# One order table for another in a fused attention and feed-forward kernel: the same operations and tiles, replayed in a new order on every engine

## Chip, cores and metric

The kernel runs on one core of a Trainium2 chip. The metric is the device time of one execution in microseconds (us), the median of several runs.

## What is computed

The inputs are q, k and v of 8 batches, 12 heads, 448 positions and 64 features, and two weights, w_in (768 x 2048) and w_out (2048 x 768), all in float32. Attention has no softmax: the scores are cut at zero, squared and divided by the sequence length. Its output, with the heads side by side, is 3584 rows of 768, and goes through a feed-forward block.

```python
def _attn_ref(q, k, v):
    S = q.shape[2]
    scale = 1.0 / np.sqrt(q.shape[-1])
    scores = scale * np.matmul(q, k.transpose(0, 1, 3, 2))
    attn = np.maximum(scores, 0.0) ** 2 / S
    return np.matmul(attn, v).astype(np.float32)

def _moe_ref(x, w_in, w_out):
    h = x @ w_in
    g = 0.5 * h * (1.0 + erf(h / np.sqrt(2.0)))
    return (g @ w_out).astype(np.float32)
```

## The kernel before

**Stages.** The work goes batch by batch, and the feed-forward work of earlier batches is laid between the attention work of later ones, so that TensorE always has some of either. All matmuls are in bf16.

- *Loads.* GpSimd's queue (POOL) loads q, k, v and the weights, casting to bf16 (`load_q` L501/L506, `add_k` L585/L588, `add_v` L608, `load_win` L521 to L523, `load_wout` L527). Its loads share eight semaphores in turn, so a load waits until the one eight places ahead has landed. w_in comes in five pieces of columns (`WINS`). The first pieces of q and k come through other queues.
- *Transposes.* For batches 0 and 1, TensorE turns q (`add_tq` L696) and k (`add_tk` L667) into PSUM tiles `tp`, and VectorE or ScalarE copies them out to `qT` and `kT` (`copy`, L548 on VectorE, L550 on ScalarE). For later batches SyncE's queue transposes by DMA.
- *Attention.* QK^T (`fn_qk`, L806, into `ps`), relu with scale (`fn_relu`, L823 on ScalarE, L825 on VectorE), square (`fn_mul`, L833 on ScalarE, L835 on VectorE), and the product with v (`add_av`, L885, into `pav`), which collects the seven blocks of 64 positions of k; its two halves are copied to `xT` (L548/L550). Batch 0 is worked in two halves of 224 positions of q, half 0 first; this shows as 64x224 matmuls. A half-width relu works on 128x448.
- *Feed-forward, first GEMM.* For half of batch 0 and a few column blocks, plain products of 12 matmuls (`add_f1`, L947, into `psh`) and a gelu (L957). For all else a seven-product scheme on 2 x 2 blocks: TensorE's products (`pe`, L1103; `pb`, L1256 for the last batch), sums of weights and of x on VectorE (`ws` L1018, `t_x` L1062), passes out of PSUM (L1141 on VectorE, L548/L550) and the gelu (L1153).
- *Feed-forward, second GEMM.* 14 groups of 256 rows (`add_group`), each with seven products in the same scheme (`pso`, L1432), sums of h on VectorE (`s_sb`), additions on VectorE into `osb` (L1466) and stores by SyncE (L1385, L1393). In the last group the last product is written in two parts, columns 0 to 255 and 256 to 383 of the half (`LAST = 256`), each with an addition and a store of its own.

Ahead of it all stand nine matmuls on zeros, 512 wide (`spin`, L1567), and a few more are put among the early work (`fill`, L1577).

**Tiles.** PSUM tiles come from two pools: `w` has three of two banks, `f` two of one bank. The bf16 attention tiles `a_sq` come from 14 buffers of pool `a`.

**What sets the order.** Every piece of work is an operation of the class `Scheduler` (`add`), numbered as it is added, with the engines that can do it. `place` replays the string `ORDER`: each word is a letter and an operation's number. P or Q puts it on TensorE, A on ScalarE, D on VectorE, G on POOL, S on SyncE, and Z places a fill. Q also changes the operation's PSUM tile: transposes take a `w` tile instead of an `f` tile, and QK^T and the product with v take two `f` tiles instead of one `w` tile. The order of the words is the order in which each engine issues its instructions. The string `HOMES` gives the buffer, in turn, that each tile of a pool takes. Waits follow from data and from buffers: an engine issues in order, and what stands behind a waiting instruction waits too.

```python
for word in ORDER.split():
    ...
        op, eng = self.open[int(word[1:])], names[word[0]]
        if word[0] == "Q":
            op.split()
    ...
    self.commit(max(self.ready(op), free), op, eng, dur, lat)
```

Of the kernel before, what the change touches and what calls it, by code (L numbers as in the profile page):

```python
# [84 lines left out]
0120120120120121210210210201201201201201201201202012010021210011021201201201021012102021021200221121  # L85
2201201201200120210210202020010212002102102102102121011001121010201012012012012010110011220112012012
021211000101201210212012021
""".replace("\n", ""),
    "f": """
0101010101010101011010101011010101010101011011010101010010101010101010101010101010101001010100110101  # L90
01010
""".replace("\n", ""),
    "a": """
0123456789abcd32105649c8b297301a546d89c723b14605ada8c91734526d0a918b652c74301abd98c6b2a50419d3879483
d174725ac60b893d271064ba53c893c210a74d3a89a37405628bc14d29a8564db03718078313d710b52a8c49670532d20985
7b137987357398a06c14d2a7359b57b259aa760814cd39b264513c807ba
# [3 lines left out]
D16 G3 G2 Q17 D18 A13 P14 D15 A19 Q20 D21 P22 D23 P45 D46 P42 A43 P39 G4 G7 P24 A40 D25 P32 D33 P36  # L100
D37 P57 A58 Z1024 Q51 A52 Q28 D41 D29 D44 Q34 D35 D59 A47 G10 Q30 A31 P54 A55 G6 P26 D27 P99 P84 A85
Z672 P69 A70 Q72 D38 D53 D56 P60 A61 D100 D62 D71 A73 G5 P48 A49 P66 D50 A67 D68 P114 A115 Q87 A88
G121 P78 A79 D116 D74 P96 D97 G8 P63 A64 G9 Q75 A65 A76 A77 P93 D94 P111 P105 A106 D112 D113 D80
D107 A95 G11 P144 A145 P108 A109 P81 A82 A83 G120 Q132 P134 D133 G12 P146 A147 D135 P167 A168 P161
A162 D86 D89 D110 P179 D180 D98 D101 P148 A149 P90 A91 D92 G129 P173 A174 D169 G125 G124 Q136 D137
Q164 A165 P102 A103 A104 D175 P117 D118 A119 P170 D171 D172 D253 P138 A139 D163 D166 D181 D254 P176
A177 D178 P245 A246 P194 A195 P185 A186 D187 P200 G123 G128 A201 P150 A151 P249 A250 P197 D198 D199
P188 A189 P191 A192 P142 P140 P203 A204 D141 G122 P182 D143 P209 A210 A183 D205 D193 D196 P215 A216
A184 P247 A248 P251 A252 P212 A213 P221 A222 G127 G126 D190 D202 P206 A207 A208 Q224 G131 P261 P278
D257 D258 P218 A279 D255 D225 A262 A219 G152 G153 Q227 A228 P268 P285 A269 D256 P264 P281 D214 A282  # L110
A265 P263 P280 D223 A211 D217 D259 P273 D260 P270 P287 G130 A220 D226 D229 D266 D286 D288 A289 Q230
A231 A232 D271 P276 P293 D283 D274 A277 A294 D374 P290 D375 D377 P378 D291 P395 A396 A379 P380 P385
P402 A275 A386 A403 A284 D376 D412 D415 P397 D400 D383 A272 P381 P398 D413 A382 P407 A399 D408 P416
P433 D434 A401 P404 P390 G240 G241 D450 P387 D391 A292 A384 D388 D405 A417 A392 A409 P419 P436 A437
A389 P423 P440 A420 A441 D414 G243 D453 D457 P410 A267 D458 P393 A411 A394 S233 P425 P442 D443 S234
Q302 A424 D426 P314 A315 A427 A303 P445 P428 P431 D429 A430 P418 D446 D451 D459 A432 Q308 A309 A444
P317 A318 P435 D438 D421 D454 P448 A449 D456 D460 D319 P462 A463 P305 A306 P311 P320 A321 A322 P464
A316 D465 P466 P468 D452 D304 D461 G155 G156 G158 G159 G239 A312 A467 S236 S235 P329 A406 A330 A313
P341 A342 D469 D455 P335 D336 D310 D307 A439 P470 D471 P472 P326 D327 S238 A447 A422 D494 S237 P368
A369 P350 A351 D495 P474 D475 P362 G242 G154 P323 G157 G160 A363 D473 D324 P344 D328 D352 A345 D346  # L120
A325 A337 D331 D496 P353 A354 D355 D497 P498 A499 P500 D501 P338 A339 D340 D343 P359 P332 A333 D334
G244 G295 G296 G297 S478 S476 A364 A360 A370 P502 D503 P504 D505 P356 A361 P347 A348 A349 D357 A358
P365 D366 D367 P506 D507 S479 P532 P523 A524 P526 D527 A533 P508 P514 D515 D516 D525 P520 A521 P371
A372 A373 D586 P529 P517 A518 A530 P510 D528 P590 A522 P607 A608 D587 D589 P597 D511 D531 P592 P614
A615 D591 D588 P609 D595 A596 G298 P593 P619 D612 P610 P626 A598 D624 P602 A611 D620 A594 P643 A627
A534 A644 G299 G300 G484 S481 S482 S483 S477 A613 D603 A604 A621 P616 P599 D617 D600 A601 P628 P645
D648 D631 D509 A618 P629 A632 D630 P622 D625 P605 P633 P650 D651 A623 A606 P646 P635 A634 S480 P547
Q538 A539 D676 A548 P655 P638 D636 D647 D519 D639 A640 P641 P652 P556 D656 A657 A557 D653 P544 D545
G487 G301 Q535 G490 G485 G486 D536 P568 G488 G489 G491 G492 A642 A654 P541 A542 D677 P658 A659 D540
D537 P680 D681 A569 A549 D678 D543 S662 D570 P565 D566 S512 P574 A575 P553 A554 A555 P682 P684 D683  # L130
A685 P550 A551 S660 S513 P562 P577 A563 A578 A649 A637 S663 S661 G666 G669 P686 D546 D558 D552 P688
D687 D689 P580 D581 P571 G493 P559 A572 A576 A560 P716 P734 A735 A561 P690 D679 P692 D579 D717 D696
D697 A567 A564 A718 D691 D699 D693 S695 P728 P722 A729 P719 A720 A723 P700 D701 P702 D721 D573 A582
P704 P740 A741 D703 P731 D732 D705 A724 P583 A584 A585 P749 D750 A736 P725 A726 A727 P708 P792 P809
D698 P794 P706 P811 D788 D733 D751 D742 D789 P799 P816 A817 A810 D730 D707 D709 P712 A793 D800 P710
D814 D791 P795 A796 D713 A815 D797 A798 P804 D711 P821 D805 P812 D813 P752 D822 A753 Q737 P743 A744
P755 A756 A757 D790 P801 P818 D819 P828 P845 A829 A823 A846 A738 A739 P830 D802 P824 P847 D826 D827
P831 P848 D850 D833 A851 A803 D832 D849 S665 S664 Q764 G672 G667 G668 G670 P835 P852 P837 P854 G671
G673 G674 A825 A806 A765 A745 P807 A808 D836 D853 D838 D855 A856 P840 P857 D841 A839 A842 D878 D858
D879 D880 P843 P860 A844 A861 P882 A859 A883 P746 A747 P773 P770 D771 D772 D766 S715 S862 S714 S864  # L140
S865 P884 D885 A774 D775 P758 S866 S863 P933 P930 A931 D754 P886 D887 A748 D934 G868 G871 G675 P888
P890 D889 D881 A834 A820 A759 D898 D891 P892 D893 S896 P927 D928 D929 P779 A935 A760 A780 D781 P761
A762 A763 P782 D783 P767 D900 D899 P902 A903 P894 D895 D932 A768 D769 A784 P776 A777 P924 D925 D926
P954 A955 A778 S867 S694 G874 G869 G870 P906 P904 D905 P936 D937 P918 A919 G872 G873 G875 A938 G876
P785 D786 D787 P921 A922 D901 P948 P908 A907 P945 A946 D992 D909 A923 P960 A956 A961 A949 P910 D911
D990 P912 P914 D920 D913 D991 D915 P994 A995 D950 P942 A943 A944 Q966 D967 P939 P957 A958 Q951 P1011
D993 P997 S1067 P1001 P1018 A1002 A1019 S916 S1065 G1070 G1073 S1064 S1066 S897 G877 D940 D941 D998
P996 D1012 P1013 D1016 D999 A1000 P1014 D1015 P1023 P1006 D1007 P1030 P1047 P1003 A1008 A968 D1024
A1025 P1032 D1048 P1049 D1028 D1052 A1031 A959 D1035 A1036 P1020 D1021 P1033 P1050 A1051 A1034 A1017
D1004 D1029 D952 D953 P1037 P1054 P1026 A1053 A1055 P1039 P1056 A1038 D1040 D1057 P1009 A1010 A1058  # L150
A1027 P1042 P1059 A1005 D1043 D1060 P1045 P1062 A1046 A1063 A1044 A1041 P1084 A1085 D1080 P969 P978
A979 D1082 P984 A985 D1081 P1086 D970 P1088 D1083 D1087 P1090 A962 A1061 A947 D1091 P972 P1138 A1139
A1022 D973 D974 D971 A986 P963 A1089 A980 P1135 A1136 P975 D964 D976 D965 P1094 D1095 P1092 D1093
P981 A982 P1144 A1145 P1126 A1127 D1100 D1101 D1137 D983 P1104 P1096 D1097 S1099 P1153 D1154 A977
P1159 A1160 P987 A988 A989 P1123 D1124 P1150 A1151 P1106 D1105 P1132 A1133 P1120 A1121 P1129 D1130
P1108 D1107 S917 D1122 D1152 D1102 D1103 D1109 D1161 A1140 A1134 A1155 P1196 P1198 P1215 P1213 A1197
D1201 A1214 P1110 S1069 G1076 S1068 S1098 G1071 G1072 P1112 D1111 D1218 A1219 D1113 A1125 D1192
D1193 P1114 G1074 G1075 G1077 D1115 D1131 D1194 A1128 P1116 D1117 P1162 A1163 D1146 P1141 A1142
D1195 P1168 D1169 Q1147 A1148 A1149 A1143 P1199 P1216 D1170 G1078 S1271 D1200 P1203 P1220 Q1186
D1217 P1156 A1204 A1221 A1187 A1157 P1222 P1205 D1230 D1164 D1206 A1202 D1223 A1224 P1225 P1208  # L160
D1209 A1210 D1226 P1232 P1249 D1250 P1228 D1231 P1234 P1251 A1233 A1188 D1237 D1254 P1235 P1252
A1229 D1253 P1211 P1239 P1256 A1227 A1238 A1255 A1212 D1236 P1241 P1258 D1240 D1242 A1158 A1207
A1257 D1259 A1243 P1180 D1181 A1260 Q1174 A1175 P1244 P1261 P1247 D1262 A1263 P1264 A1265 A1248
# [1607 lines left out]
```

## Time and profile before

| what | value |
|---|---|
| median of 3 runs | 357.82 us (357.68 to 358.1) |
| the profiled execution | 357.81 us, its span 356.04 us |
| TensorE (PE) busy | 348.8 us, 98%, 3853 matmuls |
| VectorE (DVE) busy | 305.4 us, 86% |
| ScalarE (ACT) busy | 269.0 us, 76% |
| mean granted TensorE clock | 1.000 |

The span runs from the first instruction to the last. The profile calls the engines PE (matmul), PEld (its weight loads), DVE, ACT, POOL and SP. A timeline row holds the start in us, the length in us, the engine, the line, the operation, the tiles, a count of instructions in a row (x20), and in brackets the idle time ahead with what ended it. A row by form holds the busy time in us, the mean in ns of one, and the idle time ahead.

### The profile page before, as it was taken

Reading aid. Unit: us, or ns where it says so; the run is one execution under the profiler, and the core shown is the slowest. Engines: PE = TensorE matmul, PEld = TensorE weight load, DVE = VectorE, ACT = ScalarE, POOL = GpSimd, SP = SyncE. Lnnn points to the kernel's source line nnn. Section 1 sums busy time; section 2 is a strip of 40 time slices with the busy share of each in tenths; the row PEclk is TensorE's granted clock in tenths of the full one; section 3 lists DMA queues with packets and bytes.
Section 4 is the critical chain, followed back from the end, with each engine's and each line's share of the span. In section 5 each row is a group of like instructions: output and inputs, shape, how many; then the busy total and the mean of one; then the engine's idle time right before and its main releaser. Section 6 shows DMA issues by size and latency. Waiting matters only on the chain.

```text
span 356.0 us, 9239 instructions
## 1 busy us (share of the span) xinstructions
PE 348.8 (98%) x3853; PEld 249.7 (70%) x3853; DVE 305.4 (86%) x514; ACT 269.0 (76%) x442; POOL 103.3 (29%) x138
## 2 busy tenths in 40 slices
PE   8899999999999999999999999999999999999995
PEld 4577689855589556786557965669669856888663
DVE  4999999999989998779988979898998799588662
ACT  4999987999978999498787798879986896412500
POOL 8665814195346102901093100290001000000000
PEclk9999999999999999999999999999999999999999
DMA  9999999999999956997699900799309103020222
GB/s 172 200 203 204 184 184 183 162 153 149 200 154 113 184 79 98 124 181 94 132 117 176 175 2 0 186 119 168 37 2 182 22 0 129 8 89 2 88 90 88
DMA packets 123465, 43.01 MB, mean 121 GB/s; under 512 B 100896, under 2 KB 120096, under 8 KB 123424
## 3 DMA queue, kind: packets, MB, share of 16 engines
q0 software_dynamic: 84432, 22.47, 66.9%
q1 hardware_dynamic: 38448, 19.50, 26.0%
q8 instruction: 30, 0.49, 0.6%
q10 hardware_dynamic: 544, 0.46, 0.4%
q14 instruction: 11, 0.09, 0.1%
HBM read 45.61 MB, written 11.01 MB: 159 GB/s over the span
## 4 chain that ended last, share of the span: by engine, by line
PE 93%; ACT 4%; DMA 1%; DVE 1%; issue 0%; DVEq 0%
PE pso L1432 37%; PE pe L1103 30%; PE ps L806 10%; PE pav L885 9%; PE pb L1256 5%; ACT a_sq L823 3%; PE psh L947 2%; DMA k<-in_k_dram 1%; ACT a_sq L833 1%; PE tp L667 0%; PE tp L696 0%; ACT h_sb L957 0%; DVE kT L548 0%; DVE nk L548 0%; ACT xT L550 0%
## 5 line engine op out<-in xcount | busy, mean ns | idle before, releaser
L823 ACT ACTIVATE a_sq<-ps 128x896 bf16<-128x896 f32 (+1 forms) x135 | 108.3, 863 | 9.7 <-PE ps L806 9.6
L1432 PEld LDWEIGHTS <-s_sb 128*128 128x128 bf16 x456 | 43.0, 98 | 31.5 <-issue 4.3
L835 DVE TENSOR_TENSOR a_sq<-a_sq 128x896 bf16<-128x896 bf16 x106 | 61.7, 617 | 1.7 <-ACT a_sq L823 1.0
L1103 PEld LDWEIGHTS <-win_sb 128*128 128x128 bf16 x624 | 59.2, 98 | 3.7 <-issue 2.8
L833 ACT ACTIVATE a_sq<-a_sq 128x896 bf16<-128x896 bf16 (+1 forms) x63 | 58.2, 950 | 0.9 <-DVE a_sq L825 0.6
L825 DVE TENSOR_SCALAR a_sq<-ps 128x896 bf16<-128x896 f32 (+1 forms) x51 | 50.6, 1003 | 3.4 <-PE ps L806 2.8
L1141 DVE TENSOR_TENSOR part<-pe,part 128x448 f32<-128x448 f32 x78 | 45.3, 619 | 8.0 <-PE pe L1103 7.3
L806 PE MATMUL ps<-qT,kT 64*64 64x448 bf16 (+1 forms) x756 | 49.1, 337 | 1.2 <-ACT a_sq L823 0.6
L1153 ACT ACTIVATE h_sb<-part 128x448 bf16<-128x448 f32 x78 | 42.6, 579 | 8.4 <-DVE part L1141 7.9
L1432 PEld LDWEIGHTS <-h_sb 128*128 128x128 bf16 x336 | 31.7, 98 | 23.4 <-issue 4.8
L1103 PEld LDWEIGHTS <-ws 128*128 128x128 bf16 x468 | 44.5, 98 | 2.1 <-issue 1.1
L1432 PE MATMUL pso<-wout_sb,h_sb 128*128 128x384 bf16 x224 | 41.1, 326 | 0.0
L1432 PE MATMUL pso<-t_sb,s_sb 128*128 128x384 bf16 x224 | 41.1, 326 | 0.0
L1432 PE MATMUL pso<-wout_sb,s_sb 128*128 128x384 bf16 (+2 forms) x232 | 41.0, 321 | 0.0
L588 POOL DMA_DIRECT2D nk<-in_k_dram x36 | 34.7, 969 | 11.3 <-DMA kT<-nk 5.1
L885 PE MATMUL pav<-a_sq,v_sb 64*64 64x448 bf16 (+1 forms) x756 | 36.3, 329 | 0.5 <-ACT a_sq L823 0.4
L550 ACT COPY part<-pe 128x448 f32<-128x448 f32 x52 | 26.0, 539 | 14.0 <-PE pe L1103 10.1
L806 PEld LDWEIGHTS <-kT 64*64 64x64 bf16 x756 | 19.7, 105 | 21.7 <-issue 15.2
L1103 PE MATMUL pe<-t_x,win_sb 128*128 128x224 bf16 x312 | 34.8, 259 | 0.0
L1103 PE MATMUL pe<-xT,win_sb 128*128 128x224 bf16 x312 | 34.5, 259 | 0.0
L1103 PE MATMUL pe<-t_x,ws 128*128 128x224 bf16 x312 | 34.0, 259 | 0.0
L506 POOL DMA_DIRECT2D nq<-in_q_dram x36 | 30.0, 838 | 10.8 <-DMA wout_sb<-in_moe_w_out_dram 10.3
(73 smaller groups left out, 399.3 us busy)
## 6 DMA issues: line engine op xcount, KB each, us to landing
out_dram<-osb SPq DMA_DIRECT2D x19, 384.0 KB, 2.9
nq<-in_q_dram POOLq DMA_DIRECT2D x37, 112.0 KB, 5.8
nk<-in_k_dram POOLq DMA_DIRECT2D x36, 112.0 KB, 5.0
v_sb<-in_v_dram POOLq DMA_DIRECT2D x5, 672.0 KB, 7.9
v_sb<-in_v_dram POOLq DMA_DIRECT2D x9, 224.0 KB, 7.1
win_sb<-in_moe_w_in_dram POOLq DMA_DIRECT2D x8, 192.0 KB, 9.2
wout_sb<-in_moe_w_out_dram POOLq DMA_DIRECT2D x1, 1536.0 KB, 15.2
wout_sb<-in_moe_w_out_dram POOLq DMA_DIRECT2D x4, 384.0 KB, 18.7
```

The costliest lines, as they stand in the source:

```text
L506: nc.gpsimd.dma_start(nq[b][:, g0, :, e], rows)
L588: nc.gpsimd.dma_start(nk[b][:, g0, :, e], rows[:, e].rearrange("p (i d) -> p i d", d=D))
L806: nc.tensor.matmul(side(ps, e)[64 * j : 64 * j + 64, x * w : x * w + w], kT[r, g, i * 128 + 64 * j : i * 128 + 64 * j + 64], moving, start ...
L823: A.activation(to, x, AF.Relu, scale=c_att)
L825: V.tensor_scalar(to, x, c_att, 0.0, op0=mybir.AluOpType.mult, op1=mybir.AluOpType.max,)
L833: A.activation(ar, ar, AF.Square)
L835: V.tensor_mul(ar, ar, ar)
L885: nc.tensor.matmul(side(pav[0], e)[o2 : o2 + 64, :w], vt[b][r, 2 * g + e, bass.ts(i, D)], box["a2"][r, e, o : o + w], start=(i == 0), stop ...
L1103: nc.tensor.matmul(bank[name][:, y, z * HS : z * HS + HS], w[:, k, bass.ts(mm, 128)], right()[:, k], start=first and k == 0 and z == 0, st ...
L1141: V.tensor_add(get(to), ps(name), get(other))
L1153: A.activation(h_ring()[:, m : m + 2, o + half[c].start : o + half[c].stop], src().rearrange("p (x n) -> p x n", x=2), AF.Gelu,)
L1432: nc.tensor.matmul(box[bank][:, n0:n1], left()[:, kf], right()[:, kf, n0:n1], start=bool(need) and kf == 0, stop=kf == K2 - 1, skip_group_ ...
```

## The change

The two tables `HOMES` and `ORDER` (L83 to L190) are replaced by others; no other line differs. Both orders have the same 1618 words, with the same operations; what differs is their order, the engine where two can do an operation (A or D), and the letter P or Q of a few. "Distance between packets" is a setting of the search that wrote the table, and is not in the kernel. One line of the diff:

```diff
 ORDER = """
-D16 G3 G2 Q17 D18 A13 P14 D15 A19 Q20 D21 P22 D23 P45 D46 P42 A43 P39 G4 G7 P24 A40 D25 P32 D33 P36
+G2 A13 A19 D16 P17 D18 Q20 D21 P14 D15 G3 Q22 D23 P45 P36 D46 Z672 G4 P24 D25 A37 D38 P32 A33 P42
```

Of the operations that two engines can do, 35 squares move from ScalarE to VectorE and 34 the other way, 32 relus from VectorE to ScalarE and 31 the other way, and some copies and passes. On TensorE the sequence changes 51 times from attention to feed-forward work and 51 times back, in both orders.

**VectorE's start.** The rows are the first copies of batch 0: `nk` is k in bf16, `tp` the PSUM tile of a transpose, `kT` and `qT` where it is copied to. Before:

```order
L548 CAST nk<-k_92 128x2x256
L548 COPY kT<-tp 128x512
L548 COPY qT<-tp 128x2x224
L548 COPY kT<-tp 128x384
L548 COPY kT<-tp 128x896
L825 TENSOR_SCALAR a_sq<-ps 128x2x224
```

And now:

```order
L548 CAST nk<-k_92 128x2x256
L548 COPY kT<-tp 128x512
L548 COPY kT<-tp 128x384
L548 COPY qT<-tp 128x2x224
L548 COPY kT<-tp 128x896
L825 TENSOR_SCALAR a_sq<-ps 128x2x224
```

The copy of q changed places with that of k's second part; on TensorE the transposes of that part likewise stand ahead of q's.

**ScalarE's start.** The rows run from the first relu to the first copies of `pav` to `xT`. Before:

```order
L823 ACTIVATE a_sq<-ps 128x896 x3
L823 ACTIVATE a_sq<-ps 128x448 x2
L833 ACTIVATE a_sq<-a_sq 128x2x224
L550 COPY qT<-tp 128x2x224
L823 ACTIVATE a_sq<-ps 128x896 x4
L823 ACTIVATE a_sq<-ps 128x448 x2
L550 CAST xT<-pav 128x224
L823 ACTIVATE a_sq<-ps 128x896
L823 ACTIVATE a_sq<-ps 128x2x224
L823 ACTIVATE a_sq<-ps 128x448 x2
L823 ACTIVATE a_sq<-ps 128x896
L550 CAST xT<-pav 128x224 x4
```

And now, from behind the q copy and the relus that lie ahead:

```order
L823 ACTIVATE a_sq<-ps 128x448 x2
L823 ACTIVATE a_sq<-ps 128x896 x2
L823 ACTIVATE a_sq<-ps 128x448 x2
L550 CAST xT<-pav 128x224
L823 ACTIVATE a_sq<-ps 128x896
L823 ACTIVATE a_sq<-ps 128x2x224
L823 ACTIVATE a_sq<-ps 128x896
L823 ACTIVATE a_sq<-ps 128x448 x2
L823 ACTIVATE a_sq<-ps 128x896
L823 ACTIVATE a_sq<-ps 128x448 x2
L823 ACTIVATE a_sq<-ps 128x896
L550 CAST xT<-pav 128x224 x3
```

Ahead of the last run of `xT` copies, two half-width relus (128x448 x2) have come in, the small square (L833) and one `xT` copy have gone.

**POOL's loads.** The rows are those of q and k of batch 1 (`nq`, `nk`) and the pieces of w_in behind them; 3x256 is the narrow piece, 3x512 the columns that a plain product reads next. Before:

```order
L501 DMA nq<-in_q_dram 112x4x256 x2
L585 DMA nk<-in_k_dram 128x2x448
L521 DMA win_sb<-in_moe_w_in_dram 128x3x512
L522 DMA win_sb<-in_moe_w_in_dram 64x3x512
L523 DMA win_sb<-in_moe_w_in_dram 64x3x512
L585 DMA nk<-in_k_dram 128x2x448
```

And now:

```order
L501 DMA nq<-in_q_dram 112x4x256
L521 DMA win_sb<-in_moe_w_in_dram 128x3x256
L522 DMA win_sb<-in_moe_w_in_dram 64x3x256
L523 DMA win_sb<-in_moe_w_in_dram 64x3x256
L585 DMA nk<-in_k_dram 128x2x448
L521 DMA win_sb<-in_moe_w_in_dram 128x3x512
L522 DMA win_sb<-in_moe_w_in_dram 64x3x512
L523 DMA win_sb<-in_moe_w_in_dram 64x3x512
```

The narrow piece and a load of k came ahead of the 3x512 piece.

**TensorE's end.** The rows are where the last product's two parts meet (`s_sb` is the sum of h, `pso` its PSUM tile). Before:

```order
L1432 LDWEIGHTS s_sb
L1432 MATMUL pso<-wout_sb,s_sb 128x256
L1432 LDWEIGHTS s_sb
L1432 MATMUL pso<-wout_sb,s_sb 128x128
L1432 LDWEIGHTS s_sb
```

And now:

```order
L1432 LDWEIGHTS s_sb
L1432 MATMUL pso<-wout_sb,s_sb 128x128
L1432 LDWEIGHTS s_sb
L1432 MATMUL pso<-wout_sb,s_sb 128x256
L1432 LDWEIGHTS s_sb
```

The 128-wide part moved ahead of the 256-wide one; their additions and stores follow that order.

More of the change, by code (lines that the diff above doesn't have):

```diff
@@ L105 @@
[L105 to L114, printed above, removed]
@@ L185 @@
[L185 to L187 removed]
+G2 A13 A19 D16 P17 D18 Q20 D21 P14 D15 G3 Q22 D23 P45 P36 D46 Z672 G4 P24 D25 A37 D38 P32 A33 P42
+A43 P39 D40 P51 A52 D44 D41 Z1024 Q96 A97 G6 Q26 P54 D27 P57 A58 G7 P28 D29 D47 Q34 D35 D53 A55 D56
+Q69 A70 G5 P48 G10 A49 D50 P60 A61 P114 A115 D71 P30 D31 P99 A100 D62 P66 P72 D73 D59 D74 Q93 P111
@@ new lines @@
+S1119 P1141 A1142 A1143 Q1147 P1168 A1169 D1193 D1195 P1216 P1199 D1194 D1148 D1149 P1203 P1220
+A1200 P1156 S1266 Q1186 A1221 D1217 P1222 P1205 A1157 A1202 A1219 D1204 D1223 A1224 D1206 P1208
+P1225 D1226 P1232 P1249 A1187 D1209 P1228 P1234 P1251 D1230 D1231 A1233 A1250 A1227 A1207 A1229
+D1237 D1254 P1235 P1252 D1253 A1210 A1158 A1255 P1211 A1212 P1239 P1256 D1236 P1241 P1258 D1164
+A1238 A1188 D1240 D1257 D1242 D1259 A1243 A1260 P1180 D1181 Q1174 A1175 P1244 P1261 D1262 A1263
+P1247 P1264 A1248 A1265 D1245 A1246 Q1177 D1178 D1272 D1273 D1182 P1165 A1166 D1274 D1167 P1183
@@ L188 @@
+P1499 D1560 D1514 P1563 A1562 A1495 D1551 A1552 D1497 A1498 D1500 A1501 P1565 D1564 D1556 A1535
+D1566 A1512 A1515 D1575 D1573 P1567 D1568 D1574 P1569 D1570 S1572 P1577 P1579 D1578 P1581 D1580
+A1582 P1583 P1585 D1576 D1584 D1586 P1587 D1593 D1588 D1595 S1591 D1594 S1571 P1589 D1590 P1597
+P1599 A1598 D1600 D1596 P1601 D1602 S1592 S1613 P1603 D1604 P1605 D1606 S1614 P1607 D1608 S1615
+P1610 P1609 D1612 S1617 D1611 S1616
 """
```

167 lines of the change are left out of this document (82 added, 85 removed).

## The prediction

> **What bounds the kernel now.** I read the page's first parts, then its chain, then the busy time by stage, then TensorE's timeline where a stage has gaps.
>
> ```profile
> PE 348.8 (98%) x3853; PEld 249.7 (70%) x3853; DVE 305.4 (86%) x514; ACT 269.0 (76%) x442; POOL 103.3 (29%) x138
> PEclk9999999999999999999999999999999999999999
> PE 93%; ACT 4%; DMA 1%; DVE 1%; issue 0%; DVEq 0%
> ```
>
> TensorE is busy for 98% of the span at full clock and is 93% of the chain that ended last. The remaining 7% lie somewhere, so next is the table by stage (us; then PE, PEld, DVE, ACT, POOL busy; clock; DMA share; GB/s).
>
> ```profile
> 7.10:20.20 13.10, 11.62 (x295) 7.82 (x296) 12.52 (x23) 12.57 (x23) 9.28 (x14) 1.00 1.35 200
> 20.20:46.00 25.80, 25.33 (x447) 18.80 (x445) 25.38 (x44) 24.74 (x42) 17.98 (x23) 1.00 1.43 196
> 46.00:349.60 303.60, 303.60 (x3049) 218.84 (x3047) 263.89 (x438) 229.17 (x376) 70.11 (x90) 1.00 0.90 111
> ```
>
> There are three regimes. From 46.0 to 349.6 us TensorE is busy for 303.60 of 303.60 us: no reordering of VectorE or ScalarE can take anything from there, since nothing waits. From 7.1 to 20.2 VectorE and ScalarE are the full ones (12.52 and 12.57 of 13.10) and TensorE waits for them. From 20.2 to 46.0 TensorE is idle for 0.47 us in all. After 349.6 comes the tail. So the change can gain only ahead of 46 us and in the tail; in the 303.60 it can only lose.
>
> How much can be gained ahead of 46? TensorE's timeline:
>
> ```profile
> 14.41 0.86 PE L885 MATMUL pav<-a_sq,v_sb 64*64 64x224 bf16 x28 [0.42 <-ACT a_sq L823]
> 20.16 1.32 PE L947 MATMUL psh<-xT,win_sb 128*128 128x224 bf16 x12
> 22.83 0.27 PE L947 MATMUL psh<-xT,win_sb 128*128 128x224 bf16 x1
> 23.27 1.21 PE L947 MATMUL psh<-xT,win_sb 128*128 128x224 bf16 x11 [0.17 <-DMA win_sb<-in_moe_w_in_dram]
> 24.64 0.76 PE L806 MATMUL ps<-qT,kT 64*64 64x448 bf16 x12 [0.17 <-DVE qT L548]
> 25.54 1.31 PE L947 MATMUL psh<-xT,win_sb 128*128 128x224 bf16 x12
> 28.61 1.54 PE L885 MATMUL pav<-a_sq,v_sb 64*64 64x224 bf16 x56
> 37.05 0.38 PE L806 MATMUL ps<-qT,kT 64*64 64x448 bf16 x4
> 37.26 1.49 PE L885 MATMUL pav<-a_sq,v_sb 64*64 64x448 bf16 x28
> 38.76 0.57 PE L806 MATMUL ps<-qT,kT 64*64 64x448 bf16 x8
> ```
>
> At 22.83 TensorE issues one matmul of the third plain product and then stands until 23.27 for w_in's second load. Eight loads may be in flight at once and those up to this one stand in the same queue places in both orders, so TensorE cannot pass 23.27 sooner. This is a gate: what is won ahead of it is lost there, and up to that slack a later start is absorbed. A matmul of this shape takes 0.10 start to start (twelve end 1.31 after the first starts), so of the 0.44 between 22.83 and 23.27, 0.33 is wait.
>
> Behind the gate, the removable waits are four, each found as the start less what the matmuls ahead need: 0.24 at 24.64 (eleven matmuls of 0.10 from 23.27 end their turn at 24.40; a q copy), 0.20 at 25.54 (a PSUM bank), 0.14 inside the run of 56 at 28.61, 0.16 at 38.76. Sum 0.74, which is the most that the early part can give.
>
> **The change part by part: the start.** After it TensorE transposes the second part of k ahead of q, and VectorE copies in that order.
>
> ```profile
> 5.72 0.51 ACT L550 CAST nk<-k 128x384 bf16<-128x384 f32 x1
> 5.87 0.39 PE L696 MATMUL tp<-ident,nq 112*64 112x112 bf16 x8
> 6.36 0.38 DVE L548 COPY qT<-tp 128x448 bf16<-128x448 bf16 x1
> 7.09 0.67 PE L806 MATMUL ps<-qT,kT 64*64 64x224 bf16 x20
> ```
>
> The k part is ready at 6.23 (5.72 + 0.51). Until now q's eight transposes filled the time to there, from 5.87; now they come behind six of k's, which start at 6.28, and end near 6.9; the q copy (0.38, and some 0.05 to be seen) ends near 7.35, and the first QK^T starts at 7.39 instead of 7.09: +0.30. ScalarE's first relu slips as much.
>
> Up to the last xT copy of half 0, ScalarE also gets two half-width relus more, one small square fewer and one xT copy fewer:
>
> ```profile
> L823 ACT ACTIVATE a_sq<-ps 128x448 bf16<-128x448 f32 x7 | 3.7, 656 | 0.0
> L550 ACT CAST xT<-pav 128x224 bf16<-128x224 f32 x5 | 1.8, 562 | 0.0
> L833 ACT ACTIVATE a_sq<-a_sq 128x448 bf16<-128x448 bf16 x1 | 0.6, 610 | 0.0
> ```
>
> These are pipelined, so I take them start to start: 0.41, 0.24 and 0.46 each. That is 2 x 0.41 - 0.46 - 0.24 = +0.12. With the +0.30 of the start, and about 0.1 for an AV product that now ends later, the xT chain ends some 0.5 later. The first plain product, which stands at 20.16, also waits for its bank on VectorE's xT copy rather than ScalarE's, and comes near 21.0: +0.84. At the gate 0.33 of that is absorbed: the product there ends +0.53.
>
> **Behind the gate.** Two of the four waits come from VectorE and ScalarE, whose rows there are:
>
> ```profile
> 23.97 0.61 DVE L548 COPY qT<-tp 128x896 bf16<-128x896 bf16 x1
> 24.96 0.53 ACT L957 ACTIVATE h_sb<-psh 128x448 bf16<-128x448 f32 x1
> ```
>
> The q copy ends at 24.58 and holds the QK^T of 24.64; the gelu ends at 25.49 and holds the bank of the product at 25.54. With TensorE 0.53 later, the copy is in time, and the product at 25.54 takes a bank that a copy on VectorE freed long before. So 0.24 and 0.20 of waiting vanish: +0.53 becomes +0.10 (rounded). The 0.14 of the 28.61 run and the 0.16 at 38.76 vanish too: their producers now stand ahead of other work on VectorE. 0.10 - 0.14 - 0.16 = -0.20.
>
> Against it stands one new wait. The QK^T of 37.05 takes the PSUM tile of a QK^T whose relu has moved from ScalarE to the end of a full chain on VectorE, which consists of such operations:
>
> ```profile
> 35.89 1.09 DVE L825 TENSOR_SCALAR a_sq<-ps 128x896 bf16<-128x896 f32 x1
> 38.82 2.77 DVE L835 TENSOR_TENSOR a_sq<-a_sq 128x896 bf16<-128x896 bf16 x5
> ```
>
> Since a copy near 32, two short sums, three squares (0.54 start to start, 2.77 for five), two relus and this third one (1.09 alone, 1.0 in a row) stand there, with waits for their own producers; by hand the last ends at 37.24, against a TensorE that would come at 36.85 (37.05 - 0.20): 0.41 of wait with 0.02 to see it. All of it counted, the early part is +0.21; none of it, -0.20. A chain of some ten durations by hand carries an error of that size, so I count the wait by half: **0.0** for the early part. Its ends are -0.74 (every wait gone, none new) and +0.94 (the 0.53 carried through, and the 0.41).
>
> **The loads.** POOL now brings the narrow piece of w_in (0.39 MB as written, 768 x 256) and one of k (0.23 MB) ahead of the w_in columns that a plain product behind 33 us needs.
>
> ```profile
> 30.90 0.63 POOL L522 DMA_DIRECT2D win_sb<-in_moe_w_in_dram  x1 [0.63 <-DMA win_sb<-in_moe_w_in_dram]
> 33.05 2.47 PE L947 MATMUL psh<-xT,win_sb 128*128 128x224 bf16 x24
> ```
>
> The columns landed at 30.9, which is what released that issue (it waits for the load eight places ahead); 33.05 left 2.1 of slack. 0.62 MB at the stage's 196 GB/s puts them 3.2 later, at 34.1. The product, by now second of its pair, starts near 34.1 (33.05, half of the 2.47 of both, less the 0.20). Cost **+0.1** for so close a finish; its ends are 0 (part of the 0.62 MB went beside the columns before, too) and +1.2 (each of the four more issues waiting 0.63 for its place as this row does would be 2.5; half of that).
>
> **The steady stage.** The same 3853 matmuls of the same shapes; 51 changes each way between attention and FFN on TensorE, as before; 35 squares go from ScalarE to VectorE and 34 back, 32 relus one way and 31 back. VectorE's idle 39.7 (303.60 - 263.89) and ScalarE's 74.4 hide the moved work. Cost **0**; if a producer stands too close ahead of its reader, the wait is of the order of one relu (1.09). Ends 0 and +1.1, and below nothing there is nothing, since TensorE has no idle time there.
>
> **The tail.** The last group's final product is written as a 256-wide and a 128-wide part, and now the 128-wide part comes first.
>
> ```profile
> 350.93 1.48 PE L1432 MATMUL pso<-wout_sb,s_sb 128*128 128x256 bf16 x16
> 352.45 0.62 DVE L1466 TENSOR_TENSOR osb<-pso,osb 128x128 f32<-128x128 f32 x2 [0.76 <-PE pso L1432]
> L1466 DVE TENSOR_TENSOR osb<-pso,osb 128x256 f32<-128x256 f32 x1 | 0.4, 415 | 0.0
> L1466 DVE TENSOR_TENSOR osb<-pso,osb 128x128 f32<-128x128 f32 x1 | 0.3, 291 | 0.8 <-PE pso L1432 0.8
> 352.77 0.81 SPq L1385 DMA_DIRECT2D out_dram<-osb  x2
> 353.19 0.38 SPq L1385 DMA_DIRECT2D out_dram<-osb  x1
> out_dram<-osb SPq DMA_DIRECT2D x1, 128.0 KB, 1.8
> ```
>
> VectorE's two additions run one behind the other from 352.45 to 353.07: the 128-wide (0.29) frees SyncE's first store at 352.77 (0.03 after its end at 352.74), and the 256-wide ends at 353.07 (352.45 + 0.62), whose store goes out at 353.19 behind the issue of the first, lands 1.8 later and ends the program. In the new order the 128-wide addition and its store lie beside TensorE's 256-wide matmuls. Only the 256-wide addition is left behind TensorE: 352.45 + 0.415 = 352.86, store at 352.89 with SyncE free. 353.19 - 352.89 = **-0.30**. If the store follows as late as now (0.12 after the addition), it is -0.21. The wider store was the last in both, so its 1.8 stay.
>
> **Sum.** The profiled execution took 357.81 us (span 356.04, 1.77 around it), 0.01 under the median of 357.82. 0.0 + 0.1 + 0 - 0.30 = -0.2: **357.6 us**.
>
> **The rivals.** 0.2% is 0.72 us, about what a measurement of this kernel tells from no change.
>
> *All early waits vanish and none comes* (VectorE's chain to the relu is 0.5 faster than by hand, the late start is absorbed wholly): -0.74 - 0.30 = -1.04, 356.8, faster. For it: all four causes do move. Against: the start is later by a row that can't be argued away (5.72 + 0.51).
>
> *The late start is carried past the gate*: +0.53, with the new wait of 0.41 and the tail, +0.64, 358.45: half of it slower, half the same by the bound. It decides from the xT chain's 0.5: ScalarE is at 96% there, which speaks for it; that the copy and the bank would be in time speaks against.
>
> *The w_in columns are late*: the product behind 33 us stands up to 1.2, less the 0.1 in the sum: 357.6 + 1.1 = 358.7, slower. It decides from a landing past 34.1; the load rate of the row is all that speaks here, and it gives 34.1.
>
> *A tight producer in the steady stage*: one wait of a relu's length: 357.6 + 1.1 = 358.7, slower. For it: every engine's order is new over 303 us; against: the idle 39.7 of VectorE.
>
> *TensorE's clock falls back.* At the start the clock was half:
>
> ```profile
> 0.99 4.02 PE L1567 MATMUL spin<-zero 128*128 128x512 bf16 x9 [0.99 <-DVE zero L1550]
> 8.80 0.38 PE L1577 MATMUL fill<-zero 64*64 64x512 bf16 x1
> 9.01 0.38 PE L1577 MATMUL fill<-zero 64*64 64x512 bf16 x1
> ```
>
> Nine 512-wide matmuls took 4.02, 0.45 each, where two later ones of that width follow at 0.21. A second such stretch would cost 4.02 - 9 x 0.21 = 2.1: 359.7, slower. It would need a gap longer than those of this trace, where a wait of 0.42 (14.41) leaves PEclk at 9; by my chain the new order's longest stands below 1 us. [...]
>
> *The change does not do what it says* cannot be here: the orders differ on all engines.
>
> **How the numbers follow.** Forecast 0.52 (same); all waits gone 0.20 (faster); late start carried 0.10 (0.05 same, 0.05 slower); late columns 0.10, tight producer 0.06, clock 0.02 (slower). So faster 0.20, same 0.57, slower 0.23. The range reaches from the first rival, 356.75, to 358.7, the ends of the next two; beyond it lie the clock and the worse half of late columns and producers, some 0.15 in all. The forecast's own range is 357.3 (-0.20 - 0.30) to 357.9 (+0.21 + 0.1 - 0.21).
>
> **What would show it.** In the trace after: the first QK^T at 7.4; the first plain product near 21.0; no wait for a q copy at the gate's QK^T; a wait for a relu on VectorE near 37; the product behind 33 us not named as waiting for a load; no wait between 46 us and the tail; one addition behind TensorE's end and the last store issued 0.48 after it, instead of 0.78 (353.19 less 352.41). The prediction is wrong if TensorE's 303.60 get idle time, or if the early part ends over 0.7 from where it ends now.

## The result, and the profile after

The changed kernel took **360.55 us**, the median of 22 runs (358.78 to 363.72), against 357.82 for the kernel before (22 runs): a ratio of 1.0077, 95% interval 1.0060 to 1.0094. That is slower by 2.7 us, outside the predicted range. Its runs also lie 4.9 us apart; of the kernel before's 22, all but one lie within 0.6.

The profiled execution took 359.62, one of the shorter ones, with a span of 357.8. First the page's two rows that answer to those of before, then the table by stage (us; PE, PEld, DVE, ACT, POOL busy; clock; DMA share; GB/s).

```profile
PE 348.2 (97%) x3853; PEld 249.6 (70%) x3853; DVE 308.3 (86%) x522; ACT 267.0 (75%) x435; POOL 102.2 (29%) x138
PE 77%; DMA 16%; DVE 3%; POOL 1%; issue 1%; DVEq 0%; SPq 0%
```

```profile
7.10:20.20 13.10, 10.88 (x293) 7.90 (x293) 12.11 (x24) 12.06 (x21) 9.15 (x14) 1.00 1.35 200
20.20:46.00 25.80, 25.27 (x459) 19.69 (x456) 25.50 (x44) 25.47 (x44) 17.22 (x22) 1.00 1.43 196
46.00:351.40 305.40, 304.19 (x3053) 218.18 (x3051) 267.22 (x446) 226.98 (x368) 69.68 (x91) 1.00 0.86 110
```

The chain that ended last now holds 16% of DMA where it held 1%, and the long stage, which had no idle time of TensorE, has 1.21 us of it (305.40 - 304.19). TensorE's waits from 46 to 352 us are one row (total, times, longest):

```profile
PE ps L806 <- DVE a_sq L825: 1.1, 1, 1.1
```

I set the starts of TensorE's operations side by side in the two traces, at places that the same set of operations precedes in both. The changed kernel is 0.51 late at the first QK^T, 1.02 at the first plain product, 0.25 at 43.9, 0.53 from 121 to 138, 1.81 at 140.6 and 1.80 at its end. So of the profile's 1.80, 0.25 come from the start, about 0.3 from 63 to 65, and 1.28 at one place (1.11 of it the wait in that row).

That place, on VectorE and then on TensorE:

```profile
138.96 0.56 DVE L1466 TENSOR_TENSOR osb<-pso,p_sb 128x384 f32<-128x384 f32 x1 [2.88 <-DMA out_dram<-osb]
139.44 1.08 DVE L825 TENSOR_SCALAR a_sq<-ps 128x896 bf16<-128x896 f32 x1
```

```profile
140.57 0.57 PE L806 MATMUL ps<-qT,kT 64*64 64x448 bf16 x8 [1.11 <-DVE a_sq L825]
```

The addition at 138.96 is operation 703, the first to write the next output tile `osb`. It stood 2.88 us for a store (`out_dram<-osb`) to land, since the tile takes that store's buffer. Behind it in VectorE's order stands a relu, and TensorE's QK^T needs the PSUM tile which that relu empties. In the kernel before, the same addition had no idle time ahead:

```profile
136.76 0.55 DVE L1466 TENSOR_TENSOR osb<-pso,p_sb 128x384 f32<-128x384 f32 x1
```

The output tiles have three buffers. SyncE's queue shows why one was missing, here first after, then before:

```profile
111.06 1.41 SPq L1393 DMA_DIRECT2D out_dram<-osb  x2
112.58 3.83 SPq L724 DMA_TRANSPOSE kT<-nk  x2
117.20 1.83 SPq L724 DMA_TRANSPOSE qT<-nq  x1
119.13 1.24 SPq L724 DMA_TRANSPOSE kT<-nk  x1
120.47 1.24 SPq L724 DMA_TRANSPOSE qT<-nq  x1
133.44 1.91 SPq L1393 DMA_DIRECT2D out_dram<-osb  x4
```

```profile
116.54 1.55 SPq L1393 DMA_DIRECT2D out_dram<-osb  x2
118.26 2.64 SPq L724 DMA_TRANSPOSE qT<-nq  x2
134.12 0.78 SPq L1393 DMA_DIRECT2D out_dram<-osb  x2
135.00 1.27 SPq L724 DMA_TRANSPOSE qT<-nq  x1
136.38 1.48 SPq L724 DMA_TRANSPOSE kT<-nk  x1
```

Before, a tile that was complete at 101.8 was stored at 116.5 (store 513), and operation 703 took its buffer 19 us later. In the new order that store comes at 155.8, though its tile is complete at 102.2. So operation 703 takes the buffer of a store that went out at 133.4 and 133.8 in two issues (store 694). That is 5.1 us ahead of the addition's start, and only 2.3 ahead of its turn at 136.1 (138.96 less the wait of 2.88).

The transposes of 135.0 and 136.4 moved as well, to 117.2 and 119.1. POOL's gate waits for them, and twelve loads of the next batch stand behind it. POOL after, and before:

```profile
125.11 1.92 POOL L588 DMA_DIRECT2D nk<-in_k_dram  x2
134.23 1.66 POOL L506 DMA_DIRECT2D nq<-in_q_dram  x2
```

```profile
140.21 0.71 POOL L761 COPY gate<-qT 128x16 bf16<-128x16 bf16 x1 [15.29 <-DMA qT<-nq]
140.86 1.92 POOL L588 DMA_DIRECT2D nk<-in_k_dram  x2
```

So the loads that came from 140.9 now come from 125 to 136, over the very store on which VectorE waits.

### The profile page after: what moved, and what is told of

The parts are those of the page before. It is cut to its first block, busy times and chain, and to the rows that moved or that the text cites. A ratio compares the mean times of both kernels' runs of the same rounds, so it can differ in the third digit from the quotient of the medians.

```text
span 357.8 us, 9237 instructions
## 1 busy us (share of the span) xinstructions
PE 348.2 (97%) x3853; PEld 249.6 (70%) x3853; DVE 308.3 (86%) x522; ACT 267.0 (75%) x435; POOL 102.2 (29%) x138
## 4 chain that ended last, share of the span: by engine, by line
PE 77%; DMA 16%; DVE 3%; POOL 1%; issue 1%; DVEq 0%; SPq 0%
PE pso L1432 35%; PE pe L1103 25%; PE ps L806 8%; DMA win_sb<-in_moe_w_in_dram 8%; PE pav L885 6%; DMA wout_sb<-in_moe_w_out_dram 6%; PE pb L1256 4%; DMA nq<-in_q_dram 2%; DMA out_dram<-osb 1%; DVE a_sq L825 1%; DVE osb L1466 1%; DVE part L1141 0%; POOL nk L585 0%; DVE t_sb L1366 0%; DVE s_sb L1413 0%
## 5 line engine op out<-in xcount | busy, mean ns | idle before, releaser
L823 ACT ACTIVATE a_sq<-ps 128x896 bf16<-128x896 f32 (+1 forms) x135 | 109.5, 865 | 16.1 <-PE ps L806 15.9
L835 DVE TENSOR_TENSOR a_sq<-a_sq 128x896 bf16<-128x896 bf16 (+1 forms) x107 | 62.9, 614 | 1.0 <-ACT a_sq L823 0.6
L833 ACT ACTIVATE a_sq<-a_sq 128x896 bf16<-128x896 bf16 x62 | 57.9, 960 | 0.4
L825 DVE TENSOR_SCALAR a_sq<-ps 128x896 bf16<-128x896 f32 (+1 forms) x52 | 49.8, 968 | 1.5 <-PE ps L806 1.0
L806 PE MATMUL ps<-qT,kT 64*64 64x448 bf16 (+1 forms) x756 | 48.1, 337 | 3.0 <-DVE a_sq L825 1.7
L1103 PE MATMUL pe<-t_x,ws 128*128 128x224 bf16 x312 | 35.0, 259 | 0.1
L1466 DVE TENSOR_TENSOR osb<-pso,p_sb 128x384 f32<-128x384 f32 x42 | 23.3, 554 | 12.3 <-PE pso L1432 8.5
L550 ACT COPY part<-pe 128x448 f32<-128x448 f32 x46 | 23.6, 547 | 11.8 <-PE pe L1103 7.3
```

The lines of the kernel that those rows point to most:

```text
L806: nc.tensor.matmul(side(ps, e)[64 * j : 64 * j + 64, x * w : x * w + w], kT[r, g, i * 128 + 64 * j : i * 128 + 64 * j + 64], moving, start ...
L823: A.activation(to, x, AF.Relu, scale=c_att)
L825: V.tensor_scalar(to, x, c_att, 0.0, op0=mybir.AluOpType.mult, op1=mybir.AluOpType.max,)
L833: A.activation(ar, ar, AF.Square)
L835: V.tensor_mul(ar, ar, ar)
L1103: nc.tensor.matmul(bank[name][:, y, z * HS : z * HS + HS], w[:, k, bass.ts(mm, 128)], right()[:, k], start=first and k == 0 and z == 0, st ...
```

## The experiments

The theories. **Store**: the withheld store leaves two buffers for three, and the wait for the other store's landing is the loss, with the loads beside it as what makes the landing slow. **Load** (rival): the w_out loads land later; VectorE's first subtraction on them waited 0.42 at 61.4, and two small waits of TensorE at 63 to 65 follow. **Clock** (rival): TensorE's granted clock falls. Medians are beside the kernel before's on the same chip (357.78 to 357.83).

**The same kernel again**, to see what varies.

> The changed kernel once more, unaltered. Store theory (VectorE's addition at 138.96 us, the first one into group 2's next output tile, waits for a store that was only issued at 133.4, because the other tile's store was put 39 us later; TensorE's QK^T behind it waits): 359 to 363 us again, another size of wait at 138 to 141 us in the profile, 0.5 to 4 us, and all else equal within 0.5. Load theory (the w_out loads land later, VectorE's t_sb subtraction at 61.4 waits for them, and this sets the spread): the wait at 140 stays near 1.3 and the one near 63 grows. Clock theory: the granted clock is below 1 in slices that hold no idle time of TensorE.

361.07 (359.11 to 362.46, 6 runs). Its profile is of a run of 362.37. VectorE, then TensorE and the stages behind it:

```profile
140.03 0.56 DVE L1466 TENSOR_TENSOR osb<-pso,p_sb 128x384 f32<-128x384 f32 x1 [4.26 <-DMA out_dram<-osb]
```

```profile
141.64 0.57 PE L806 MATMUL ps<-qT,kT 64*64 64x448 bf16 x8 [2.49 <-DVE a_sq L825]
```

```profile
141.50:142.90 1.40, 1.26 (x13) 0.64 (x13) 1.40 (x4) 0.28 (x1) 0.00 (x0) 1.00 2.39 161
142.90:146.00 3.10, 3.10 (x15) 1.76 (x14) 2.14 (x4) 2.74 (x4) 0.00 (x0) 0.51 1.03 64
```

The store landed 6.9 us after its issue instead of 5.5, the wait grew from 1.11 to 2.49, and 1.3 us behind it the clock fell to half (0.51). So the clock theory's sign is there, but as the wait's consequence. It isn't the main loss either: of the changed kernel's 22 runs, sixteen had a granted clock of 0.998 or more and still took 358.8 to 361.9. TensorE comes out of this place 4.5 late at the end, 0.2 of it from ahead of it. In the first profile, behind the wait of 1.11, the clock stands at 1.00. The waits at 63 to 65 are absent here, so they too depend on when a load lands, but they aren't needed for the loss.

**The store moved early**, one word:

```diff
-... P688 S512 G666 ... G674 S714 S867 S863 S513 S862 ...
+... P688 S512 S513 G666 ... G674 S714 S867 S863 S862 ...
```

> The changed kernel with one word moved: the late store (S513) stands right behind the store ahead of it on SyncE's queue (S512), 39 us earlier. Store theory: no wait near 140 in the profile, span 1.3 shorter than the 357.8 of the changed kernel's profile (356.5), time 358.2 to 358.6, and the runs within 0.6 of each other. Load theory: 359.5 to 361 with the spread unchanged. Clock theory: as the changed kernel, 360.5.

358.42 (357.64 to 361.32, 11 runs; ratio 1.0020, 0.9995 to 1.0044). In VectorE's row the addition now waits for its product only:

```profile
136.47 0.56 DVE L1466 TENSOR_TENSOR osb<-pso,p_sb 128x384 f32<-128x384 f32 x1 [0.30 <-PE pso L1432]
```

TensorE has no wait over 0.11 us from 46 us on. By the medians, one word gives back 2.1 of the 2.7 us. The expected spread of 0.6 was wrong: nine of the eleven runs lie within 1.4, two at 360.6 and 361.3. No profile was taken of such a run.

**The w_out loads in their former order besides** (`G241 G240` to `G240 G241`).

> The same with two load words changed places besides (G240 ahead of G241, as before the change): w_out's large piece is issued ahead of the two small ones. Store theory with the loads as the second cause: the waits of 0.17 and 0.25 near 63 and 65 us vanish, 357.8 to 358.2. Store theory alone: as the run with the store moved, within 0.2. Load theory: this is the one that gives back most, 358.

358.85 (357.34 to 362.20, 12 runs), no better than without. Three of its runs lie at 359.9, 361.4 and 362.2, with a granted clock of 0.985 to 0.993, so the early store 513 doesn't end the spread. Neither profile has the waits at 63 to 65, so the order of these loads isn't what made them. The load theory falls as a main cause.

**The same store held back in the kernel before**, one word:

```diff
-... S660 S513 P562 ... A741 D703 P731 ...
+... S660 P562 ... A741 D703 S513 P731 ...
```

> The kernel before with one word moved: the same store (S513) comes behind the addition (D703) that takes the next output tile, so that this addition takes the tile of the store issued at 134.1 instead. Store theory: VectorE stands 2 to 3 us at 136.8 for that store, TensorE waits behind it, 358.5 to 361 with a spread of over 1 us. Load theory and clock theory: 357.8, no wait, spread 0.3.

358.42 (358.08 to 358.76; ratio 1.0017, 1.0008 to 1.0026): +0.6, less than expected and with little spread. VectorE waited 0.94, since the store landed 3.7 us after its issue, not 5.5 or 6.9.

```profile
137.77 0.56 DVE L1466 TENSOR_TENSOR osb<-pso,p_sb 128x384 f32<-128x384 f32 x1 [0.94 <-DMA out_dram<-osb]
```

So the withheld store alone isn't the loss. The next two runs test the loads.

**Both halves put into the kernel before**: the store late, and the two transposes ahead of the store of 134, which lets POOL's loads come early.

```diff
-... D693 S695 P728 ... A741 D703 P731 ... S665 S664 Q764 ...
+... D693 S665 S664 S695 P728 ... A741 D703 S513 P731 ... Q764 ...
```

> The kernel before with both halves of the cause put in: the store S513 behind the addition D703, as in the run with the late store, and the two transposes S665 and S664 ahead of the store S695, so that POOL's batch loads come at 125 to 136 us, as in the changed kernel. If the late store costs little by itself (0.6) and much beside the loads: VectorE stands 2 to 4 us for the store, TensorE 1 to 2.7, 359 to 361.5 with a spread of over 1. If the loads don't matter: 358.4, as with the late store alone.

361.92 (360.82 to 363.19, 6 runs; ratio 1.0105, 1.0072 to 1.0139), more than the whole change, and above the expected 361.5. Five of the six runs have a granted clock of 0.995, the profiled one (362.00) among them. VectorE, TensorE, and the stages:

```profile
139.71 0.56 DVE L1466 TENSOR_TENSOR osb<-pso,p_sb 128x384 f32<-128x384 f32 x1 [2.65 <-DMA out_dram<-osb]
```

```profile
141.32 0.38 PE L806 MATMUL ps<-qT,kT 64*64 64x448 bf16 x4 [2.00 <-DVE a_sq L825]
```

```profile
141.50:144.50 3.00, 2.92 (x18) 1.86 (x15) 2.64 (x5) 1.87 (x2) 0.00 (x0) 0.70 0.00 0
144.50:147.50 3.00, 3.00 (x21) 2.30 (x20) 2.25 (x5) 0.00 (x0) 0.00 (x0) 0.73 0.00 0
```

Three words of 1618, in the kernel before, make a loss larger than that of the whole change, with a spread of 2.4 us. With the loads, a late store costs 4.1 us, some 1.8 of it by the clock; without them, 0.6. The early loads without the late store were not run in the kernel before; in the changed kernel with its store early they cost VectorE no wait at this place.

**The converse: in the changed kernel, the two transposes put back behind the stores**, the store left late (`S665 S664` moved behind `S695`).

> The changed kernel, with two of SyncE's transposes (S665 and S664, keys and queries that are first used at 157 us) put back behind the two stores of 133 to 135 us, where they stood before the change. They open POOL's gate for twelve batch loads, so these loads come near 141 instead of 125 to 136. The late store stays late. If the store's slow landing (5.5 to 6.9 us after its issue) comes from those loads: it lands about 3.6 after its issue, as in the run with the store late in the kernel before; VectorE stands near 1 us for it, TensorE 0 to 0.3, the time is 358.3 to 358.8 and the spread under 1. If the store alone is the cause: 359 to 363, as the changed kernel.

361.20 (360.01 to 364.52, 6 runs): not the time that I expected, though the place behaved as expected. The addition waited 0.55, since the store landed 3.2 us after its issue, and TensorE not at all. But the next batch's loads came later too, at 166.7 to 177.4 instead of 163.4 to 175.3, and met the next tight store: issued at 177.7, it landed 5.9 us later, where that of the changed kernel, issued at 179.7, landed after 2.5. VectorE, then TensorE:

```profile
183.60 0.56 DVE L1466 TENSOR_TENSOR osb<-pso,p_sb 128x384 f32<-128x384 f32 x1 [3.18 <-DMA out_dram<-osb]
```

```profile
184.21 1.46 PE L1432 MATMUL pso<-wout_sb,s_sb 128*128 128x384 bf16 x8 [1.31 <-DVE osb L1466]
```

The same thing a second time: two more stores (715 and 896) go out 35 and 21 us after their tiles are complete, so the addition at 183.60 takes a buffer whose store was issued at 177.7, 2.7 us ahead of the addition's turn. TensorE waits another 0.76 at 186.75.

**The start put back**, with the store early: the first load of k ahead of making the identity on POOL, and q's transposes and copy ahead of k's second part.

```diff
-G2 A13 A19 D16 P17 D18 Q20 D21 P14 D15 G3 Q22 ...
+G3 G2 A13 A19 D16 P17 D18 P14 D15 Q20 D21 Q22 ...
```

> The changed kernel with the store moved early (as in the first run of that), and its first words put back besides: POOL issues the first load of k ahead of making the identity, and TensorE and VectorE take q's transposes and copy ahead of k's second part. If the remaining spread of the run with the early store (357.6 to 359.0) comes from the landing of that first load: first QK^T at 7.1 in the profile without a wait for a load, 357.6 to 358.0 and the spread 0.5. If it lies elsewhere: median 358.4 and spread as there.

357.57 (357.12 to 358.81, 12 runs; ratio 0.9997, 0.9986 to 1.0008): 0.85 less than with the store alone, the first QK^T at 7.11. The spread is 1.7, not 0.5. So the late start is a second, smaller cause; the two intervals overlap, but the pair of runs with all stores early, below, shows it again (0.5). In the six profiles with the new start that QK^T stood at 7.14 to 8.12, for the order of the transposes and for k's load, which POOL issued at 1.42 instead of 1.25:

```profile
7.09 0.58 PE L667 MATMUL tp<-ident,nk 128*64 128x128 bf16 x14 [0.40 <-DMA nk<-in_k_dram]
7.60 0.48 PE L806 MATMUL ps<-qT,kT 64*64 64x224 bf16 x12
```

These rows are the changed kernel's first profile.

**All three put back.**

> All three put back: the store early, the two transposes behind the stores, the start as before. Store and load collision as the cause of the loss: 357.5 to 357.9, within 0.2% of the kernel before, and spread 0.5, since the rest of the new order is worth about -0.2 to 0 by the profiles so far. If the new order costs something else in the steady stage: over 358.5.

359.28 (357.85 to 360.16, 10 runs): not the 357.5 to 357.9 that I expected, and worse than without the later loads. VectorE waited 1.61 for a store at 181.95 and TensorE 0.57 behind it, at the second tight place; a product at 33.9 lost 0.27 besides. It agrees with the run of the later loads: neither of the two places of the loads that were tried is good while stores are held back.

**All four withheld stores moved early** (513, 715, 896, and 916, which was held 81 us), each right behind the store or addition ahead of it, first with the new start, then with the former one.

> The changed kernel with all four stores that its order holds back 19 to 81 us (S513, S715, S896, S916) put right behind the store or addition ahead of them, so that each next output tile finds a buffer whose store was issued over 9 us earlier. Store theory: no wait of VectorE for a store in the profile, neither at 137, nor at 181, nor at 227; the runs over 359 of the kernel with one store moved are gone, the rest (the landing of the first loads) stays: 357.6 to 358.4, median 357.9. If the spread of the one-store kernel came from elsewhere: runs up to 361 remain.

> The same, with the start of the kernel before put back too. Store theory and the start as the two causes: 357.2 to 357.7, all runs within 0.6, median 357.4, which is 0.3 to 0.5 under the kernel before (the new order's steady stage is 0.2 to 0.4 shorter in the profiles without such waits). If something else of the new order costs time: 357.8 or more.

358.11 (357.54 to 359.82; ratio 1.0010, 0.9990 to 1.0029) and 357.62 (357.26 to 358.38; ratio 0.9991, 0.9973 to 1.0010). Neither profile has a wait for a store on VectorE from 100 to 300 us, or one on TensorE from 46 us to the tail. The spread shrank (2.3 and 1.1 us, from 3.7 with one store moved) but not to the 0.6 that I expected. What varies in the rest stays open. The last version is the best, 0.2 under the kernel before, which its interval does not tell from no change.

**The tail**, in the kernel before: the wide product with its addition and store, then the narrow one with its own.

```diff
-P1609 P1610 D1612 S1617 D1611 S1616
+P1609 D1611 S1616 P1610 D1612 S1617
```

> The kernel before with its last six words in another order: the 256-wide product, its addition and store, then the 128-wide product, its addition and store. If a wait is taken on the PSUM tile as a whole (the theory for why the tail gained nothing): TensorE stands for VectorE's addition, about 0.5, before the 128-wide product, and the end comes 0.0 to 0.2 later, 357.8 to 358.0. If on the part that is written: the wider addition lies beside TensorE, only the 128-wide one and its store are left, 0.4 earlier, 357.4.

357.95 (357.67 to 358.11; ratio 1.0002, 0.9994 to 1.0010).

```profile
351.83 0.42 DVE L1466 TENSOR_TENSOR osb<-pso,osb 128x256 f32<-128x256 f32 x1 [0.32 <-PE pso L1432]
352.31 0.61 PE L1432 MATMUL pso<-wout_sb,s_sb 128*128 128x128 bf16 x8 [0.52 <-DVE osb L1466]
352.95 0.29 DVE L1466 TENSOR_TENSOR osb<-pso,osb 128x128 f32<-128x128 f32 x1 [0.70 <-PE pso L1432]
```

TensorE stands 0.52 for the addition, though it writes other columns: the wait goes by the whole PSUM tile (which is one bank here, so the run doesn't tell a tile from a bank). What the end gains, the product loses.

**A probe of the clock**, in the kernel before: the addition of operation v2 (the first into an output tile) is issued several times over in groups 9 to 13, with the same result.

```diff
+REP = {9: 7, 10: 6, 11: 8, 12: 10, 13: 5}
...
-                    V.tensor_add(
-                        out()[:, n0:n1], box[bank][:, n0:n1], other()[:, n0:n1]
-                    )
+                    for _ in range(rep):
+                        V.tensor_add(
+                            out()[:, n0:n1], box[bank][:, n0:n1], other()[:, n0:n1]
+                        )
```

> The kernel before, where in groups 9 to 13 of the second GEMM one addition of VectorE is issued 7, 6, 8, 10 and 5 times over (same operands, same result), so that TensorE's next product stands for some 1.9, 1.4, 2.4, 3.3 and 1.0 us. The changed kernel's profiles showed full clock behind a wait of 1.28 and half clock for some 3 us behind one of 2.66. Theory that a wait of about 2 to 2.7 is enough: half clock behind the two or three longest, full behind 1.0 and 1.4. [...]

One run, 378.25. The waits came out longer than meant: 2.73, 2.16, 2.91, 4.73 and 1.71. TensorE at four of them (line numbers are one or two higher in this kernel), and the row of its waits for that addition (total, times, longest), which has the fifth (by the idle time of the stages 0.59 ahead of 350 us and 4.14 behind it):

```profile
294.53 2.72 PE L1433 MATMUL pso<-wout_sb,s_sb 128*128 128x384 bf16 x8 [2.73 <-DVE osb L1468]
315.43 1.31 PE L1257 MATMUL pb<-xs,win_sb 128*128 128x224 bf16 x12 [2.16 <-DVE xs L1221]
338.53 2.72 PE L1433 MATMUL pso<-wout_sb,s_sb 128*128 128x384 bf16 x8 [2.91 <-DVE osb L1468]
367.45 0.81 PE L1433 MATMUL pso<-wout_sb,s_sb 128*128 128x384 bf16 x4 [1.71 <-DVE osb L1468]
```

```profile
PE pso L1433 <- DVE osb L1468: 12.1, 4, 4.7
```

Behind 2.73 and 2.91, eight matmuls of 384 columns take 2.72; at full clock they take 1.46. Behind 2.16 twelve of 224 take 1.31, as ever, and behind 1.71 four of 384 take 0.81, at full clock. By stages of 5 us, the granted clock was 0.91 and 0.75 from 290, 1.00 and 1.00 from 310 (the wait of 2.16), 0.84 and 0.82 from 335, 0.71 and 0.61 from 350 (the wait of 4.73), and 1.00 from 365. So the theory's "about 2 to 2.7" isn't a bound on the wait's length: 2.16 lies within it and did nothing.

## Why the prediction was wrong, step by step

*The steady stage* is the step that failed. It said that VectorE's 39.7 us of idle time and ScalarE's 74.4 hide the moved work, at cost 0 and at most +1.1 for a producer close ahead of its reader. I had listed the moves of squares and relus, and not those of SyncE's stores and transposes. Idle time of an engine hides nothing when an instruction at the head of its queue waits for a DMA, as VectorE's addition did here for 2.88, and TensorE behind it for 1.11. I looked for producers of data. What came too close was the freeing of a buffer: operation 703 and the store whose buffer it takes, 5.1 us apart instead of 19 (2.3 at its turn, without the wait). Which buffer it takes could be read from the order of the stores, and that a store can land late from the trace of before, where the landings take 1.5 to 7.7 us; that the loads would be what delays this one took the runs. That the end of +1.1 equals the first profile's wait of 1.11 is chance: it was the length of a relu, for another mechanism. It was too low for the runs, where in the profiles the wait goes from 1.1 to 2.5 and the clock adds to it.

*The clock rival* had a chance of 0.02 and came true in six of the 22 runs, by their granted clock of 0.988 to 0.995. Its price was 2.1; it measured 1.7 in the repeat (TensorE 2.9 late at the wait's end and 4.5 late behind the half clock) and 1.8 in the kernel before with both halves (TensorE 3.97 later for a wait that held it 2.2 of that). The reason against it, that no gap of the new order is over 1 us, fell with the chain that lacked this wait. Waits of 2.00, 2.49, 2.73, 2.91 and 4.73 were followed by half clock here, each once, and one of 2.16 was not. So the length of a wait alone doesn't tell, and what else decides was not shown.

*The start* was right in kind. The first plain product was put at 21.0 and stood at 21.18, the first QK^T at 7.39 and stood at 7.60, 0.40 of wait for k's load among it. That load's issue, 0.17 later by POOL's first two words, I had not seen, and what follows from it varies: the first QK^T stood at 7.14 to 8.12 in six profiles of this start. The gate at 23.27 isn't fixed either, since it hangs on a landing: the kernel before with both halves ran the third plain product from 23.02 without a wait, and the repeat of the changed kernel waited 0.2 in it for w_in's load, until 24.09. The waits for the q copy and for the bank vanished as foretold, and the new wait for the relu of 37 us was 0.25 by the profile, where I put 0.41 and counted half. At 43.9 TensorE was 0.25 late, where the sum had 0.0 and its ends were -0.74 and +0.94. Two small sums of the working are off by 0.02, which changes nothing: 0.84 less 0.33 is 0.51 and not 0.53, and 357.81 less 1.04 is 356.77 and not 356.75.

*The w_in columns* landed in time in the changed kernel: the product, at 33.17, shows no wait for a load, as forecast, and the 0.1 that the sum had for it was not seen. In the run with all three put back the same pair of products stood 0.27 at 33.9; that trace doesn't name what it waited for, so a late load is not ruled out there.

*The tail* gained nothing: 3.63 us from TensorE's end to the span's end in both (357.84 - 354.21 and 356.04 - 352.41), where the sum had -0.30.

```profile
352.73 1.48 PE L1432 MATMUL pso<-wout_sb,s_sb 128*128 128x128 bf16 x16
354.25 0.62 DVE L1466 TENSOR_TENSOR osb<-pso,osb 128x128 f32<-128x128 f32 x2 [0.76 <-PE pso L1432]
```

Both additions still come behind TensorE's last matmul. The working took it that the narrow one waits for its own part; in this order it stands behind both products, and the run on the tail shows that the tile is what is waited for.

By the medians, the store's place accounts for 2.1 (360.55 to 358.42) and the start for 0.85 (358.42 to 357.57), or 0.5 with all stores early (358.11 to 357.62); what is left of the new order is worth -0.2, which no interval here tells from nothing.

## What to carry to other kernels

When an order changes, make one table for each ring of buffers: which earlier tile frees the buffer that each new tile takes, and how old its store or read is by then. Counted from the store's last issue to the addition's start, the changed kernel's first profile has six ages of 3.2 to 5.1 us, where those of before are all but one (4.8) above 5.5. Only one of the six cost a wait there, and a second (operation 905, at 3.2) did in the runs where loads came just ahead of its store. So the table says where to look, not what it costs. The order alone gives the buffers; the ages of a new order have to be estimated from the trace of before. A saturated engine with no waits at all is not safe for that: a late store, cheap by itself (+0.6), and loads let loose 15 us sooner, which cost nothing that shows where the store was moved early, made 4 us together. And if a changed kernel's runs spread more than those of before, look first for a wait on a DMA's landing.

## What the runs showed of the hardware

- TensorE's clock halved (0.51 from 142.9 to 146.0 in the repeat) in or behind waits of 2.00, 2.49, 2.73, 2.91 and 4.73 us in the middle of a busy stretch. From the granted clock of the stages I estimate, with each drop taken as one stretch at half, that it lasted about 3.4 us behind each of the first four and 6.8 behind 4.73. In the probe, eight matmuls of 384 columns took 2.51 and 2.52 us from the first start to the next operation's behind 2.73 and 2.91, and 1.30 at full clock. Waits of 1.11, 1.71 and 2.16 didn't do it. So the length alone doesn't decide; the wait of 2.00 made TensorE 3.97 us late, nearly twice itself.
- The drop came at no fixed time. Estimated from the same stages, it came 1.4 and 1.3 us after the work resumed behind 2.00 and 2.49, but some 0.4 and 0.1 us before that behind 2.73 and 2.91. What sets it these runs don't show.
- The store that VectorE's addition takes its buffer from (128 rows, issued at 132.8 to 134.3 us) landed 3.2 and 3.7 us after its issue with no batch loads beside it (the later loads, and the late store in the kernel before). Beside POOL's batch loads it landed after 5.4 (both halves in the kernel before) and after 5.5 and 6.9 in two profiles of the changed kernel, where the addition waited 2.88 and 4.26 for it; a kernel that waits for it has that as part of its spread.
